# When q, k, v and the first expert's weights are loaded: in step order, or as early as buffers allow

## The chip, the cores and the metric

The kernel runs on one core of a Trainium2 chip. The metric is the device time of one launch in microseconds (us). The core has five engines, each with its own instruction stream: TensorE (PE in the profile), VectorE (DVE), ScalarE (ACT), GpSimd (POOL) and SyncE (SP). Transfers run on 16 DMA engines, which serve several queues. [...] The DMA transposes and the stores of the output are issued by SyncE (queue q1).

## The reference, cut to what matters

A block-sparse attention (a sorting network mixes the blocks of k and v) is followed by a mixture of experts whose gates are normalised in both directions.

```python
# attention: B=4, H=8, S=768, D=64, 8 blocks of 96 rows; P starts as sort_net
for _ in range(5):
    P = exp(P - max(P, -1)); P = P / (sum(P, -1) + 1e-9); P = P / (sum(P, -2) + 1e-9)
k_sorted = einsum('bhij,bhjcd->bhicd', P, k_b)
v_sorted = einsum('bhij,bhjcd->bhicd', P, v_b)
scores = matmul(q_b, k_sorted^T) / sqrt(D)          # inside each block
attn   = exp(scores - max); attn = attn / sum(attn)
x      = matmul(attn, v_sorted)                     # -> [3072, 512]

# experts: E=8, F=1024
P = exp(x @ w_gate - max)
for _ in range(8):
    P /= P.sum(1) + 1e-9;  P /= P.sum(0) + 1e-9;  P *= N / E
out = sum over e of  P[:, e] * (relu(x @ w1[e]) @ w2[e])
```

## The kernel before, in words

**Heads and pairs.** The 32 heads (4 batches of 8) are worked one after the other. q, k and v are loaded by pairs of heads: `load_pair(n)` (L65 to L73) takes a pair's buffer out of the pool `rawp`, which has six, and issues three DMAs of 192 KB each (bfloat16) from GpSimd, for k, v and q. `relayout(n)` (L75) reorders the pair's k and v on GpSimd into one of two `kv` buffers. `q_transpose(n)` (L253) turns q on TensorE into `qT_`.

**One step per head.** The loop at L399 goes over steps s = 0 to 33. Step s holds, in the order in which they are written: on even steps `build_R` for heads s+4 and s+5 (GpSimd, the sorting weights); `scores(s)`, on TensorE, with the maximum and the subtraction on VectorE (L327, L332, L334); the transpose of head s-1's weights on TensorE, with a copy on ScalarE (L349, L351); `sort_kv(s+2)`; `weights(s)`, the exponential on ScalarE (L338); on even steps `q_transpose(s//2+1)` and `relayout(s//2+2)`; `x_transpose` of a finished pair; `attend` of head s-1 (of head s-2 from head 16 on) with `normalise` (L356, L364, L365); the loads that the table `loads` names for this step; and, at s = 2, `load_expert(0)`.

**The ring around v.** `sort_kv(g)` (L306) sorts k and v of head g on TensorE, copies them to `kvT_` on ScalarE (L315), and SyncE issues a DMA transpose (L318) that writes v into `v1_`. `kvT_` has three buffers and `v1_` has five. The copy of head g+3 may start only when the transpose of head g has landed, and `attend(g)` needs that transpose too.

**Order.** The program is written out by hand (`manual_schedule`): each engine runs its own instructions in the order of the text. An instruction that waits holds back everything behind it on its engine. For GpSimd this means that loads, `build_R` and `relayout` stand in one queue. In front of the loop the kernel loads pairs 0 to 4 (L88 to L92), and after `relayout(1)` pair 5 and the gate's weights (L386, L387). The table (L396, L397) loads pairs 6 to 10 at steps 1, 3, 5, 7 and 9, and pairs 11 to 15 at steps 10, 11, 13, 15 and 17.

**The experts.** When a batch of heads is done, pieces of the gate and of expert 0's two layers (`gate_piece`, `l1_piece` L192, `l2_piece` L203) are put between the steps' work by `fill()`. The first pieces are added at the end of step 9 and run from step 10 on, so w1 of expert 0 is first read at 57.9 us and w2 at 67.3 us. Until step 8 the gaps on TensorE get `keep_warm` matmuls (L273) of no use to the result. After the heads come the rest of expert 0, the normalisation of the gates and experts 1 to 7 (L460, L538), from 186 us to the end.

Of the kernel before, what the change touches and what calls it, by code (L numbers as in the profile page):

```python
# [12 lines left out]
BF16 = mybir.dt.bfloat16  # L13
# [11 lines left out]
def kernel(  # L25
# [11 lines left out]
    nc = tc.nc  # L37
# [4 lines left out]
    N, Dm, E, F = 3072, 512, 8, 1024  # L42
# [22 lines left out]
    def load_pair(n):  # L65
        kv = rawp.tile([128, 2, 2, CL, D], BF16, name="kvr")
        qr = rawp.tile([128, 2, CL, D], BF16, name="qr")
        for t, r in ((k, kv[:, 0]), (v, kv[:, 1]), (q, qr)):
            nc.gpsimd.dma_start(
                out=r.rearrange("p h c d -> p h (c d)"),  # L70
                in_=bass.AP(tensor=t.tensor, offset=t.offset + 2 * n * S * D,
                            ap=[[CL * D, 128], [S * D, 2], [1, CL * D]]))
        raw_t[n] = (kv, qr)  # L73

    def relayout(n):  # L75

        kv = iop.tile([128, 2 * CL, 2, D], BF16, name="kv")
        nc.gpsimd.tensor_copy(kv.rearrange("p c t d -> p t c d"),  # L78
                              raw_t[n][0].rearrange("p t h c d -> p t (h c) d"))
        kv_t[n] = kv  # L80
# [8 lines left out]
    load_pair(1)  # L89
    load_pair(2)  # L90
    load_pair(3)
    load_pair(4)  # L92


    P9 = pp.tile([32, 9, 9], F32)
# [65 lines left out]
    wp = ctx.enter_context(tc.tile_pool(name="wp", bufs=2))  # L161
    wg = ones.tile([128, 4, E], BF16)
    w1t, w2t = [], []

    def load_expert(e):
        w1e = wp.tile([128, 4, F], BF16, name="w1e")
        w2e = wp.tile([128, 8, Dm], BF16, name="w2e")
        nc.gpsimd.dma_start(out=w1e, in_=moe_w1[e].rearrange("(kk k) f -> k kk f", k=128))  # L168
        nc.gpsimd.dma_start(out=w2e, in_=moe_w2[e].rearrange("(fb k) f -> k fb f", k=128))
        w1t.append(w1e)  # L170
        w2t.append(w2e)

    xtp = ctx.enter_context(tc.tile_pool(name="xtp", bufs=1))
    xtT = xtp.tile([128, 4, N], BF16)
# [63 lines left out]
    def fill():  # L238
        if slots[0] > 0:
            ahead[0] += sum(c for c, _ in pieces) / slots[0]  # L240
            slots[0] -= 1
        while pieces and ahead[0] >= pieces[0][0] / 2:
            c, run = pieces.pop(0)
            run()
            ahead[0] -= c
# [7 lines left out]
    def q_transpose(n):  # L253


        qr = raw_t[n][1]
        tq = psF.tile([128, 2, CL // 2, 128], BF16, name="psF")
        for e in range(2):
            for c in range(CL // 2):
                nc.tensor.matmul(tq[:, e, c], qr[:, e, 2 * c:2 * c + 2].rearrange("p l d -> p (l d)"),  # L260
                                 Ibf, is_transpose=True, start=True, stop=True)
        for e in range(2):
            to = qT_[0:64, n % 2, e, 0:S].rearrange(
                "p (i c l h) -> p l c i h", i=NB, l=2, h=CH)
            for l in range(2):
                (nc.vector.tensor_copy if e == 0 and n > 1 else nc.scalar.copy)(  # L266
                    to[:, l], tq[64 * l:64 * l + 64, e].rearrange("p c (i h) -> p c i h", h=CH))

    def keep_warm(n):

        w = psF.tile([128, 512], F32, name="psF")
        for i in range(n):
            nc.tensor.matmul(w[:, (i % 4) * 128:(i % 4 + 1) * 128], Ibf, Ibf, start=True, stop=True)  # L273
# [22 lines left out]
    def build_R(eng, src, g0, n):  # L296
        eng.tensor_tensor(
            out=R[:, g0:g0 + n],
            in0=mkap(src, [src.ap[0], [1, n], [32, 8], [0, CH]], off=g0),
            in1=mkap(mask16, [mask16.ap[0], [0, n], [0, 8], [1, CH]]),  # L300
            op=ALU.mult)
# [4 lines left out]
    def sort_kv(g):  # L306

        kv, e = kv_t[g // 2], g % 2
        kvps = psB.tile([128, 2, 512], F32, name="psB")
        kvf = mkap(kvps, [kvps.ap[0], [1, CL * 128]])  # L310
        for cl in range(CL):
            nc.tensor.matmul(kvf[:, cl * 128:(cl + 1) * 128],  # L312
                             kv[:, e * CL + cl].rearrange("p t d -> p (t d)"),
                             R[:, g].rearrange("p i c -> p (i c)"), start=True, stop=True)
        nc.scalar.copy(kvT_[:, g % NKT, :, 0:96].rearrange("p i (l c) -> p i l c", c=CH),  # L315
                       mkap(kvps, [kvps.ap[0], [CH, NB], [128, CL], [1, CH]]))

        nc.sync.dma_start_transpose(  # L318
            out=v1_[:, g % NVB, :, 0:64],
            in_=kvT_[64:128, g % NKT].rearrange("p i c -> p (i c)"))  # L320

    def scores(g):

        qT, kvT = qT_[:, (g // 2) % 2, g % 2], kvT_[:, g % NKT]
        sps = psB.tile([128, 2, 512], F32, name="psB")
        for i in range(NB):
            nc.tensor.matmul(sps[:, i // 4, (i % 4) * 96:(i % 4 + 1) * 96],  # L327
                             qT[:, i * BL:i * BL + 128], kvT[:, i, 0:96],
                             start=True, stop=True)
        s4 = sps[0:96, :, 0:384].rearrange("p a (i c) -> p a i c", c=96)  # L330
        mx = sp.tile([96, 2, 4], F32, name="mx")
        nc.vector.reduce_max(out=mx, in_=s4, axis=AX.X)  # L332
        ssb = sp.tile([96, 2, 4, 96], F32, name="ssb")
        nc.vector.tensor_sub(ssb, s4, mkap(mx, [mx.ap[0], [4, 2], [1, 4], [0, 96]]))  # L334
        ssb_t[g] = ssb

    def weights(g):
        nc.scalar.activation(out=at_[:, g % NAT, :, 0:96],  # L338
                             in_=ssb_t.pop(g).rearrange("p a i c -> p (a i) c"),
                             func=AF.Exp, scale=scale)  # L340
        if g in DT:
            nc.sync.dma_start_transpose(
                out=aT_[:, g % NTT, 0:S].rearrange("p (i c) -> p i c", c=BL),
                in_=at_[:, g % NAT].rearrange("p i c -> p (i c)"))

    def a_transpose(g):
        ta = psF.tile([128, NB, 96], BF16, name="psF")
        for i in range(NB):
            nc.tensor.matmul(ta[:, i, :], at_[:, g % NAT, i], Ibf[0:96, 0:96],  # L349
                             is_transpose=True, start=True, stop=True)  # L350
        nc.scalar.copy(aT_[0:97, g % NTT, 0:S], ta[0:97].rearrange("p i c -> p (i c)"))  # L351
# [31 lines left out]
    keep_warm(10)  # L383
    build_R(nc.gpsimd, Pb, 2, 2)
    relayout(1)
    load_pair(5)  # L386
    nc.gpsimd.dma_start(out=wg, in_=moe_w_gate.rearrange("(kk k) e -> k kk e", k=128))  # L387
    NP = NH // 2
    step = {g: g + (2 if g in DT else 1) for g in range(NH)}
# [3 lines left out]
    x_step = {}  # L393
    for n in range(NP):
        x_step.setdefault(max(step[2 * n], step[2 * n + 1]) + 1, []).append(n)
    loads = {2 * n - 11: n for n in range(6, 11)}  # L396
    loads.update({10: 11, 11: 12, 13: 13, 15: 14, 17: 15})  # L397
    new = []
    for s in range(NH + 2):  # L399
        if s % 2 == 0 and s + 4 < NH:  # L400
            build_R(nc.gpsimd, Pb, s + 4, 2)
        if s < NH:
            scores(s)
        if s == 0:
            sort_kv(1)
            onesc = ones.tile([128, 128], F32)
            nc.gpsimd.memset(onesc, 1.0)
            nc.gpsimd.memset(glog[:, NT, :], EPS / 128)
            nc.gpsimd.memset(glog[:, 0:NT, E:E + 1], EPS)
        fill()  # L410
        if s < 9:
            keep_warm(4)
        if 0 <= s - 1 < NH and s - 1 not in DT:
            a_transpose(s - 1)
        fill()
        if s + 2 < NH:
            sort_kv(s + 2)
        if s < NH:
            weights(s)
        if s % 2 == 0:  # L420
            if 0 < s and s // 2 + 1 < NP:
                q_transpose(s // 2 + 1)
            if s // 2 + 2 < NP:
                relayout(s // 2 + 2)
        for n in x_step.get(s, []):
            x_transpose(n)
            if n % 4 == 3 and n < NP - 1:
                new = [(0.7, gate_piece(n // 4))] + batch_pieces(n // 4)
        fill()
        if s < 9:  # L430
            keep_warm(6)
        for g in at_step.get(s, []):
            attend(g)
            normalise(g)
        if s in loads:
            load_pair(loads[s])
        fill()
        if new:
            add(new, {9:34,17:40,26:28}[s])
            new = []  # L440
        if s == 2:
            load_expert(0)
        if s == 31:

            late_ = pp.tile([1, 8], BF16)
            nc.gpsimd.tensor_copy(late_, at_[0:1, 31 % NAT, 0, 0:8])
            load_expert(1)
# [57 lines left out]
    for it in range(8):  # L505
# [8 lines left out]
            out=gl, in0=gl, scalar=float(N) / E,  # L514
# [5 lines left out]
    for e in range(1, E):  # L520
        if e + 1 < E:
            load_expert(e + 1)
        for nc4 in range(6):
            for fb in range(AHEAD if (e, nc4) == (1, 0) else 0, 8):
                l1_tile(e, nc4, fb)
            for tt in range(4):
# [8 lines left out]
                for c0 in range(0, Dm, W):  # L535
                    oacc = psF.tile([128, Dm], F32, name="psF")
                    for fb in range(8):
# [3 lines left out]
                        out=osbl[:, t, c0:c0 + W], in0=oacc[:, 0:W],  # L541
                        scalar=glog[:, t, e:e + 1], in1=osbl[:, t, c0:c0 + W],
                        op0=ALU.mult, op1=ALU.add)
                    if e == E - 1:
                        nc.sync.dma_start(out=out[t * 128:(t + 1) * 128, c0:c0 + W],
                                          in_=osbl[:, t, c0:c0 + W])
# [30 lines left out]
```

## Time and profile before

| what | us |
|---|---|
| median of 3 runs (760.49, 761.14, 768.26) | 761.14 |
| the profiled execution's own time | 764.39 |
| its span, first to last instruction | 762.6 |
| TensorE busy in the span | 736.4 (97%) |
| VectorE, ScalarE, GpSimd busy | 268.5, 331.9, 80.7 |
| first scores of head 0 (L327) | 15.8 |
| first piece of expert 0 (L192) | 57.9 |
| experts 1 to 7 from | 186 |

All times of places are counted from the start of the span of the profiled execution. A page of the profile shows busy times by engine, the span in 40 slices with the busy share of each in tenths, the DMA queues, the chain of work that ended last (followed back from the last instruction, each step to what released it), and groups of instructions. A row of the timeline has start, length, engine, line, operation, output and inputs, and, in brackets, how long the engine was idle before it and what ended that. In rows of a queue, the first number counts packets, the second is MB moved, the third the time that its packets took as a share of 16 engines.

### The profile page before, as it was taken

The page shows a single profiled execution, that of the slowest core. Times are in us where ns is not written, and L with a number is a line of the kernel's source. Part 1 is how long each engine was busy: PE and PEld are TensorE (multiplying, and loading weights), DVE is VectorE, ACT ScalarE, POOL GpSimd, SP SyncE. Part 2 cuts the span into 40 slices and gives each one's busy share as a digit, 9 for nine tenths or more (in the row PEclk, how much of TensorE's full clock was granted, in tenths as well). Part 3 has the DMA queues.
Part 4 walks back from the last instruction along what each step waited for, and adds up shares of the span by engine and source line. Part 5 has one row for each costly group of instructions (what it writes and reads, how often), then busy time and mean ns, then how long its engine had stood idle before and what let it go on. Part 6 is the DMA issues. An engine that isn't in the chain of part 4 may idle for free.

```text
span 762.6 us, 10716 instructions
## 1 busy us (share of the span) xinstructions
PE 736.4 (97%) x4509; PEld 375.3 (49%) x4509; DVE 268.5 (35%) x462; ACT 331.9 (44%) x559; POOL 80.7 (11%) x105
## 2 busy tenths in 40 slices
PE   6669999999999999999999999999999999999998
PEld 5657666655444444444444444444444444444444
DVE  5777888556512112122121221221212212112122
ACT  7778887744342332423424324233243342332422
POOL 8855430000000000000000000000000000000000
PEclk9999999999999999999999999999999999999999
DMA  9999656345100420015000700042001500002112
GB/s 151 159 176 179 110 91 81 61 86 91 21 1 1 74 37 1 0 28 83 1 0 1 111 0 1 1 65 46 1 0 20 92 0 1 1 1 96 70 70 96
DMA packets 58431, 40.15 MB, mean 53 GB/s; under 512 B 30608, under 2 KB 51344, under 8 KB 58384
## 3 DMA queue, kind: packets, MB, share of 16 engines
q0 software_dynamic: 26128, 26.23, 23.4%
q1 hardware_dynamic: 32256, 13.25, 8.5%
q8 instruction: 35, 0.57, 0.3%
q14 instruction: 12, 0.10, 0.0%
HBM read 52.45 MB, written 6.29 MB: 77 GB/s over the span
## 4 chain that ended last, share of the span: by engine, by line
PE 90%; DMA 4%; ACT 3%; DVE 2%; issue 1%; ACTq 0%; DVEq 0%
PE psF L538 38%; PE hps L460 38%; PE psF L203 5%; PE psF L192 5%; DMA v__108<-kvT__106 4%; PE psB L327 1%; ACT qT__111 L266 1%; PE psB L356 1%; PE psB L312 1%; ACT kvT__106 L315 1%; DVE ssb L334 1%; PE psF L349 0%; PE psF L374 0%; DVE mx L332 0%; PE psF L214 0%
## 5 line engine op out<-in xcount | busy, mean ns | idle before, releaser
L463 ACT ACTIVATE hTs<-hps 128x512 bf16<-128x512 f32 x336 | 200.8, 598 | 372.8 <-PE hps L460 372.8
L460 PE MATMUL hps<-xtT,w1e 128*128 128x512 bf16 x1344 | 297.4, 379 | 0.0
L538 PE MATMUL psF<-w2e,hTs 128*128 128x512 bf16 (+1 forms) x1352 | 296.9, 378 | 0.0
L540 DVE SCALAR_TENSOR_TENSOR osbl<-psF,glog,osbl 128x512 f32<-128x512 f32 (+1 forms) x169 | 126.3, 748 | 437.5 <-PE psF L538 437.4
L538 PEld LDWEIGHTS <-hTs 128*128 128x128 bf16 x1352 | 132.3, 98 | 157.8
L460 PEld LDWEIGHTS <-w1e 128*128 128x128 bf16 x1344 | 131.5, 98 | 158.5
L192 PE MATMUL psF<-xtT,w1e 128*128 128x384 bf16 x256 | 49.0, 325 | 0.6 <-ACT qT__111 L266 0.6
L168 POOL DMA_DIRECT2D w1e<-in_moe_w_dram x8 | 6.1, 767 | 394.3 <-PE hps L460 370.4
L203 PE MATMUL psF<-w2e,hTs 128*128 128x512 bf16 x192 | 45.4, 379 | 0.0
L195 ACT ACTIVATE hTs<-psF 128x384 bf16<-128x384 f32 x64 | 29.7, 499 | 7.4 <-PE psF L192 6.8
L315 ACT CAST kvT__106<-psB 128x768 bf16<-128x768 f32 x32 | 25.9, 808 | 16.1 <-issue 7.1
L332 DVE TENSOR_REDUCE mx<-psB 96x8 f32<-96x768 f32 x32 | 30.4, 949 | 5.3 <-PE psB L327 5.0
L334 DVE TENSOR_TENSOR ssb<-psB,mx 96x768 f32<-96x768 f32 x32 | 30.5, 954 | 3.2
L192 PEld LDWEIGHTS <-w1e 128*128 128x128 bf16 x256 | 22.9, 98 | 12.7 <-issue 1.0
L338 ACT ACTIVATE at__114<-ssb 96x768 bf16<-96x768 f32 x32 | 27.3, 853 | 2.0 <-DVE ssb L334 2.0
L203 PEld LDWEIGHTS <-hTs 128*128 128x128 bf16 x192 | 17.9, 100 | 17.0
L78 POOL COPY kv<-kvr 128x1536 bf16<-128x1536 bf16 x15 | 22.0, 1469 | 34.1 <-PE psB L312 17.5
L356 PE MATMUL psB<-v__108,aT__115 97*128 97x65 bf16 x256 | 13.1, 195 | 10.5 <-ACT kvT__106 L315 5.7
L365 DVE TENSOR_TENSOR og__309<-psB,den 96x512 bf16<-96x512 f32 x32 | 22.0, 687 | 1.1
L273 PE MATMUL psF<-Ibf 128*128 128x128 bf16 x169 | 16.7, 254 | 4.1 <-ACT Ibf L150 4.1
L356 PEld LDWEIGHTS <-aT__115 97*128 97x128 bf16 x256 | 11.7, 99 | 14.9 <-issue 12.2
L327 PE MATMUL psB<-kvT__106,qT__111 128*128 128x96 bf16 x256 | 16.5, 208 | 2.0 <-ACT kvT__106 L315 1.5
(84 smaller groups left out, 296.4 us busy)
## 6 DMA issues: line engine op xcount, KB each, us to landing
w1e<-in_moe_w_dram POOLq DMA_DIRECT2D x8, 1024.0 KB, 7.9
w2e<-in_moe_w_dram POOLq DMA_DIRECT2D x8, 1024.0 KB, 8.8
out_dram<-osbl SPq DMA_DIRECT2D x23, 256.0 KB, 2.0
kvr<-in_k_dram POOLq DMA_DIRECT2D x16, 192.0 KB, 8.1
kvr<-in_v_dram POOLq DMA_DIRECT2D x16, 192.0 KB, 8.7
qr<-in_q_dram POOLq DMA_DIRECT2D x16, 192.0 KB, 9.1
v__108<-kvT__106 SPq DMA_TRANSPOSE x32, 4.2
out_dram<-osbl SPq DMA_DIRECT2D x2, 128.0 KB, 1.7
```

Of the source, the lines that this page charges most:

```text
L192: nc.tensor.matmul(hps[:, 0:HC], w1t[0][:, kk, fb * 128:(fb + 1) * 128], xtT[:, kk, c * HC:(c + 1) * HC], start=(kk == 0), stop=(kk == 3))
L195: nc.scalar.activation(out=hT0[c][:, fb, 0:HC], in_=hps[:, 0:HC], func=AF.Relu)
L203: nc.tensor.matmul(oacc, hT0[c][:, fb, tt * 128:(tt + 1) * 128], w2t[0][:, fb, :], start=(fb == 0), stop=(fb == 7))
L315: nc.scalar.copy(kvT_[:, g % NKT, :, 0:96].rearrange("p i (l c) -> p i l c", c=CH), mkap(kvps, [kvps.ap[0], [CH, NB], [128, CL], [1, CH]]))
L332: nc.vector.reduce_max(out=mx, in_=s4, axis=AX.X)
L334: nc.vector.tensor_sub(ssb, s4, mkap(mx, [mx.ap[0], [4, 2], [1, 4], [0, 96]]))
L338: nc.scalar.activation(out=at_[:, g % NAT, :, 0:96], in_=ssb_t.pop(g).rearrange("p a i c -> p (a i) c"), func=AF.Exp, scale=scale)
L356: nc.tensor.matmul(ops_[:, i // 4, i % 4, 0:65], aT_[0:97, g % NTT, i * BL:i * BL + 128], v1_[0:97, g % NVB, i, 0:65], start=True, stop=True)
L460: nc.tensor.matmul(hps, w1t[e][:, kk, fb * 128:(fb + 1) * 128], xtT[:, kk, nc4 * 512:(nc4 + 1) * 512], start=(kk == 0), stop=(kk == 3))
L463: nc.scalar.activation(out=hT[e, nc4][:, fb, :], in_=hps, func=AF.Relu)
L538: nc.tensor.matmul(oacc[:, 0:W], hT[e, nc4][:, fb, tt * 128:(tt + 1) * 128], w2t[e][:, fb, c0:c0 + W], start=(fb == 0), stop=(fb == 7))
L540: nc.vector.scalar_tensor_tensor(out=osbl[:, t, c0:c0 + W], in0=oacc[:, 0:W], scalar=glog[:, t, e:e + 1], in1=osbl[:, t, c0:c0 + W], op0=A ...
```

## The change

Only the times of issue are changed. Pair 4 is loaded at step 2 instead of in front of everything, pair 5 at step 4 instead of before the loop. Pairs 6 to 10 are loaded at steps 6, 7, 8, 9 and 9 instead of 1, 3, 5, 7 and 9. Pairs 11 to 15 keep their steps. Expert 0's w1 is loaded at the end of step 1 and its w2 at the end of step 7, where both were loaded at the end of step 2. Buffers, sizes and all other instructions stay.

```diff
     load_pair(3)
-    load_pair(4)
...
+    def load_w1(e):
+        w1t.append(wp.tile([128, 4, F], BF16, name="w1e"))
+        nc.gpsimd.dma_start(out=w1t[e], in_=moe_w1[e].rearrange("(kk k) f -> k kk f", k=128))
+
+    def load_w2(e):
+        w2t.append(wp.tile([128, 8, Dm], BF16, name="w2e"))
+        nc.gpsimd.dma_start(out=w2t[e], in_=moe_w2[e].rearrange("(fb k) f -> k fb f", k=128))
+
     def load_expert(e):
-        w1e = wp.tile([128, 4, F], BF16, name="w1e")
-        w2e = wp.tile([128, 8, Dm], BF16, name="w2e")
-        nc.gpsimd.dma_start(out=w1e, in_=moe_w1[e].rearrange("(kk k) f -> k kk f", k=128))
-        nc.gpsimd.dma_start(out=w2e, in_=moe_w2[e].rearrange("(fb k) f -> k fb f", k=128))
-        w1t.append(w1e)
-        w2t.append(w2e)
+        load_w1(e)
+        load_w2(e)
...
     relayout(1)
-    load_pair(5)
     nc.gpsimd.dma_start(out=wg, in_=moe_w_gate.rearrange("(kk k) e -> k kk e", k=128))
...
-    loads = {2 * n - 11: n for n in range(6, 11)}
-    loads.update({10: 11, 11: 12, 13: 13, 15: 14, 17: 15})
+    loads = {2: [4], 4: [5], 6: [6], 7: [7], 8: [8], 9: [9, 10], 10: [11], 11: [12], 13: [13], 15: [14], 17: [15]}
...
-        if s in loads:
-            load_pair(loads[s])
+        for n in loads.get(s, ()):
+            load_pair(n)
         fill()
...
-        if s == 2:
-            load_expert(0)
+        if s == 1:
+            load_w1(0)
+        if s == 7:
+            load_w2(0)
```

## The prediction

> **What bounds the kernel now.** I read the page's slices first, then the chain of work that ended last.
>
> ```profile
> PE   6669999999999999999999999999999999999998
> ...
> DMA  9999656345100420015000700042001500002112
> ...
> PE 90%; DMA 4%; ACT 3%; DVE 2%; issue 1%; ACTq 0%; DVEq 0%
> ```
>
> One slice is 19 us. From the fourth slice on TensorE is full. In the first three it is at 0.6 while the DMA engines are at 0.9 or more. So the time is that of reaching the full stretch, plus TensorE's work from there. Between 57 and 186 us TensorE is busy for 126.20 of 129 us, and its waits there sum to some 4 us with no DMA among them. What is saved ahead of 57 us therefore reaches the end whole. The chain over 0 to 57 us, its longest pieces:
>
> ```profile
> 15.77 7.74 DMA v__108<-kvT__106
> ...
> 24.44 10.45 DMA v__108<-kvT__106
> ...
> 35.82 11.86 DMA v__108<-kvT__106
> ```
>
> Columns: start, length, what. These 30.05 us are three of the DMA transposes that line 318 issues, one per head, from SyncE. They lie on the chain because `kvT_` has three buffers: the copy of head g+3 (L315) waits until the transpose of head g has landed. The rows of L318 for 15 to 60 us and for 91 to 141 us, in this order, say what a transpose costs beside loads and without them:
>
> ```profile
> DMA to landing us min/median/max: 7.7/9.1/12.6
> ...
> DMA to landing us min/median/max: 2.5/2.5/4.4
> ```
>
> The queues in 34 to 36 us (expert 0's w1 is on the wires) and in 57 to 59 us (q, k, v loads), two lines each:
>
> ```profile
> q0 software_dynamic: 177, 0.36, 96.1%
> q1 hardware_dynamic: 153, 0.04, 15.3%
> ...
> q0 software_dynamic: 393, 0.28, 90.4%
> q1 hardware_dynamic: 389, 0.10, 36.7%
> ```
>
> First number: packets. Loads (q0) and transposes (q1) pass nearly one packet for one. From 15.5 to 87 us, q1 has 9792 packets for 18 transposes, 544 each. Beside loads they pass at 195 per us, so 2.8 us per transpose; beside w1 at 77 per us, 7.1 us; beside w2 (463 packets in 40 to 43 us) 3.5 us. A head goes by in about 3.3 us where nothing waits for a DMA, so beside loads that never pause the transposes only just keep up, and w1 puts them behind. The floor of a head is VectorE's:
>
> ```profile
> 28.58 0.20 DVE L364 RECIPROCAL den<-psB 96x8 f32<-96x8 f32 x1 [0.51 <-PE psB L356]
> ...
> 31.61 0.20 DVE L364 RECIPROCAL den<-psB 96x8 f32<-96x8 f32 x1 [0.19 <-PE psB L356]
> ...
> 35.47 0.20 DVE L364 RECIPROCAL den<-psB 96x8 f32<-96x8 f32 x1 [0.38 <-PE psB L356]
> ...
> 41.66 0.20 DVE L364 RECIPROCAL den<-psB 96x8 f32<-96x8 f32 x1 [3.27 <-PE psB L356]
> ```
>
> From one `den` to the next is one head: 3.03 us where VectorE hardly waits, 3.86, and 6.19 where it waits. With the two q copies (0.71 us, every second head) the same is 3.51 us (from 49.07 to 52.58), then 3.08. Floor: 3.05 and 3.5, in turn.
>
> **The change, part by part.**
>
> *What goes from the front.* The three loads of pair 4 leave the prologue and those of pair 5 leave the place after `relayout(1)`. Pair 3's q lands at 19.2 us with no load behind it but wg. Transpose 0, issued at 15.77, then finds free wires after 19.2 rather than loads until 23.5. I let it land at 20 to 22. Its two waiters move: the copy of head 3 (began 23.62, cannot begin before the ACT copy of 20.80 ends at 21.6) and the attend of head 0 (began 23.65, cannot begin before that copy either, 21.65). `den` of head 0 stood at 24.09; it becomes 22.1 at best, 22.9 if the wires stall as they do here.
>
> *The steps from there.* `den` of heads 0 to 8 now: 24.09, 28.58, 31.61, 35.47, 41.66, 45.35, 49.07, 52.58, 55.66. The differences are 4.49, 3.03, 3.86, 6.19, 3.69, 3.71, 3.51, 3.08. Against 3.5 and 3.05 in turn they are over by 1.0, 0, 0.35, 3.15, 0.2, 0.65, 0, 0: 5.35 us. With 1.2 to 2.0 at head 0 the most that can be gained is 6.6 to 7.4 us. What is late next is VectorE, so nothing beyond this is to be had without shorter steps.
>
> *w1 earlier.* It is issued at step 1 instead of step 2. POOL's queue: R and `relayout(1)` to 16.7, wg to 17.4 (pair 5's 2.2 us are gone), R, memsets and `relayout(2)` to 19.8, w1 there instead of at 26.03. Its row later in the kernel says 7.9 us to landing: about 28. From some 21.6 its packets meet whatever is left of transposes 1 and 2 (issued at 18.10 and 19.48), at 7.1 us per transpose. If those two are through by then, nothing is lost; if both are still whole, they land near 28.5 and 31, against copies due at about 25.5 and 28.5: 3 us lost. No row shows which. I take 0.9 us, nearer to nothing, because with free wires from 19.2 us two transposes need little more than what 24 to 28 us shows (1069 q1 packets there, two transposes, beside loads); range 0 to 3.
>
> *Loads in step order, and POOL.* Load n now stands behind `relayout(n-1)` on POOL, and that waits for the landing of n-1. With w1 landed at 28, pair 4's v lands at 30.2, `relayout(4)` (1.47 us) ends at 31.7; `sort_kv(8)` at step 6 wants it at 36.7. Load 5 is issued at 31.7, its v lands some 4.3 us after its issue (the second load of the kernel, from an empty queue) or a little more, `relayout(5)` ends near 38, due 43.2. Loads 6 and 7 and w2 are issued from 38 to 43.2, `relayout(6)` ends at 45.4, due 51.5. No engine waits; the slack is 5 us each time. The q halves land 5 us ahead of `q_transpose` (pair 4: 31.5 against 37).
>
> *w2 later.* The first use of w2 (L203) was at 67.31, so near 61 now. w2 goes out at 42.4 behind six loads of about 1.3 us each from 39.7, and takes some 7 us (46.66 less 39.1 here): landed at 54.5. Here POOL pays:
>
> ```profile
> 39.39 0.76 POOL L69 DMA_DIRECT2D kvr<-in_k_dram  x1 [0.35 <-DMA w1e<-in_moe_w_dram]
> 46.95 0.72 POOL L69 DMA_DIRECT2D kvr<-in_v_dram  x1 [6.80 <-DMA w2e<-in_moe_w_dram]
> ```
>
> A POOL load waits for the landing of the POOL load eight before it. That stall held back `relayout(6)` here. Counted in the new order, v of pair 10 is eight behind w2: it goes out at 54.6, q of pair 10 at 55.8, then R (0.66) and `relayout(7)`, which ends near 58.3. `sort_kv(14)`, 66.48 here, wants it at 60.1. Slack 1.8 us, cost nothing; if w2 lands 3 us later, 1 to 2 us are lost. I take 0.
>
> **The sum.** 7.3 (nearly the most) less 0.9 for w1: 6.4 us. The profiled execution took 764.39 us, its span 762.6, 1.8 around it; by its own time the result is 758.0. It lies 3.25 over the median of the runs, 761.14. The stretch in question has the same order in every run, so I take the 6.4 from the median: **754.7**.
>
> **Rivals.**
>
> *More than the floor* (a gain over 7.6, 753.5 or less). The floor rows themselves hold waits of 0.2 to 0.5 us, and TensorE's granted clock is 0.85 to 0.87 from 15.8 to 49 us against 1.00 later; steps of 2.95 and 3.4 would add 1 us. For: these waits; against: VectorE's own work is 2.8 us plus 0.71. Chance 0.25, 753.
>
> *w1 in the way of the first transposes, or `relayout(7)` late* (above): 2.5 to 4 us less. 758. Chance 0.18.
>
> *The wires stay as full.* All bytes remain, and what falls in steps 1 to 9 (w1, w2, pairs 4 to 7) is some 27 us of wire in 26 us. For it: beside loads a transpose still takes 2.8 us. Against: until now nine pairs and both weights ran in that time, and a pause of 2 us lets a backlog pass. Gain under 2: 761. Chance 0.07.
>
> *Loads too late: slower.* The place is the POOL chain landing, relayout, next load. The landing of v after its issue decides. At L us, `relayout(5)` ends at 33.8 + L, due 43.2, and `relayout(6)` at 36.0 + 2L, due 51.5: it bites from L = 7.7. In 47 to 61 us the loads took 9.4 to 12.1, median 10.4. At 10.4 `relayout(5)` is 0.8 late, `relayout(6)` a further 4.5, and w2, then landed at 67, holds `relayout(7)` until 71, a further 5.6: 10.9 late less the 6.4 is 4.5 slower, 765.6. Those rows had up to eight loads ahead in the queue, here there are two or three at most, so L is nearer to 5. Chance 0.09, and about half of it would be over 1%, with a landing of 12.
> [...]
>
> *The forecast* (a gain of 5 to 7.6): 0.41.
>
> **Range and chances.** 1% (7.6 us) is about what a measurement of this kernel can tell from no change. The forecast lies inside it, so "within 1%" holds the forecast, the second and third rival and half of the slower one: 0.69. Faster by over 1%: 0.25. Slower by over 1%: 0.06. The range leaves out a tenth at each end: the floor beaten by 1 us (752.5), and the late loads (above 761).
>
> **What would show it.** The chain no longer has transposes of 8 to 12 us in 15 to 48 us; copies L315 hardly wait for them; `den` steps at 3.0 and 3.5 from head 1 on; the first L192 at about 51.5 instead of 57.9; TensorE's clock at 1.00 there. Wrong would be: POOL's L78 copies ending later than the matmuls of L312 ask for, a wait of L312 on POOL, L203 waiting for w2, or transposes 1 to 3 landing after 28 us.

## The result, and the profile after

The changed kernel takes 764.73 us (median of 22 runs), the kernel before 761.71 us beside it: a ratio of 1.0034, 95% interval 1.0019 to 1.0049. It is slower by 0.3%. The prediction was 754.7 us, with a range from 752.5 to 761.0.

The profiled execution of the change took 764.50 us, with a span of 762.7. The slices of its page, and the shares of its chain:

```profile
PE   6778999999999999999999999999999999999998
...
DMA  9999945345100420015000600042001500002112
...
PE 90%; DMA 4%; ACT 3%; DVE 2%; issue 1%; POOL 1%; ACTq 0%; DVEq 0%; POOLq 0%
```

TensorE is fuller in the second and third slice (0.7 and 0.7, where before had 0.6 and 0.6) and emptier in the fourth (0.8, where before had 0.9), and the span is that of before. The DMA engines are busy for 0.9 of the fifth slice (76 to 95 us), where before had 0.6: the loads now have a fuller tail, which comes back below. At the front the transposes came sooner, as was expected, though some still took 8 to 10 us. Time to landing of the transposes of v issued from 15 to 50 us, before and after:

```profile
DMA to landing us min/median/max: 7.7/9.3/12.6
```

```profile
DMA to landing us min/median/max: 2.5/6.4/10.1
```

The rows of `den` on VectorE (L367 in the changed kernel), heads 8 to 11. First number: start.

```profile
49.04 0.20 DVE L367 RECIPROCAL den<-psB 96x8 f32<-96x8 f32 x1 [0.23 <-PE psB L359]
...
55.38 0.20 DVE L367 RECIPROCAL den<-psB 96x8 f32<-96x8 f32 x1 [0.72 <-PE psB L359]
...
59.59 0.20 DVE L367 RECIPROCAL den<-psB 96x8 f32<-96x8 f32 x1 [1.20 <-PE psB L359]
...
69.82 0.19 DVE L367 RECIPROCAL den<-psB 96x8 f32<-96x8 f32 x1
```

Head 8 comes at 49.04, where it came at 55.66. Head 11, at 69.82, is later than before (69.68). The 6.6 us are lost between heads 8 and 11. The chain of the change there (start, length, what):

```profile
41.69 5.55 DMA kvr<-in_v_dram
...
47.40 1.41 POOL kv L78
48.80 12.99 DMA kvr<-in_k_dram
...
62.82 0.66 POOL R L300
63.48 1.41 POOL kv L78
...
64.94 0.68 PE psB L315 x6
```

and the same on GpSimd's timeline, with TensorE's row behind it:

```profile
45.24 0.95 POOL L170 DMA_DIRECT2D w2e<-in_moe_w_dram  x1
...
53.71 0.72 POOL L69 DMA_DIRECT2D kvr<-in_k_dram  x1 [0.55 <-DMA qr<-in_q_dram]
60.66 0.71 POOL L69 DMA_DIRECT2D kvr<-in_v_dram  x1 [6.23 <-DMA w2e<-in_moe_w_dram]
62.09 0.71 POOL L69 DMA_DIRECT2D qr<-in_q_dram  x1 [0.71 <-DMA kvr<-in_k_dram]
62.82 0.66 POOL L300 TENSOR_TENSOR R<-Pb,mask 128x256 bf16<-128x256 f32 x1
63.41 1.47 POOL L78 COPY kv<-kvr 128x1536 bf16<-128x1536 bf16 x1
```

```profile
64.94 0.68 PE L315 MATMUL psB<-R,kv 128*128 128x128 bf16 x6 [3.40 <-POOL kv L78]
```

v of pair 10 waits on GpSimd for w2's landing (issued at 45.24, 15.13 us to landing, so 60.37), and q of pair 10 for the landing of k of pair 8 (issued at 48.80, 12.99 us, so near 61.8). Behind them stand R and `relayout(7)`, and behind that `sort_kv(14)`: TensorE idles for 3.40 us. Then a second loss, in TensorE's clock. Rows of the change: stretch, its length, TensorE's busy time (instructions), granted clock, DMA share, GB/s.

```profile
48.06:51.47 3.41, 1.86 (x49) 1.00 1.32 183
51.47:54.89 3.42, 3.42 (x20) 0.50 1.26 184
...
61.71:65.13 3.42, 0.19 (x4) 1.00 1.30 196
65.13:68.54 3.41, 3.41 (x18) 0.50 1.31 197
```

In both cases a stretch in which TensorE was not full (1.86 and 0.19 of 3.4 us) is followed by 3.41 us at half clock, and TensorE was full there, so that the loss is half of that by estimate, 1.7 us. From head 8 to head 9 it was 1.66 us (6.34 where before took 4.68), and after the idle time at 61 to 65 us about as much again. Sum: 6.62 less 1.66 is 4.96, 5.03 at head 10; less 3.40 and some 1.8, nothing is left at head 11.

One more thing has to be known to read the medians. The first profiled execution of before (764.39 us) lay 2.7 us over its median. The kernel before was therefore profiled a second time (below): 762.33 us, span 760.6. There head 8 comes at 52.11:

```profile
52.11 0.20 DVE L364 RECIPROCAL den<-psB 96x8 f32<-96x8 f32 x1 [0.24 <-PE psB L356]
```

So the lead of the change at head 8 is 3.1 us and not 6.6. It is still 3.05 us at head 10 (62.64 against 59.59), because this execution has a stretch of half clock of its own from 54.81 to 58.22. All of it is lost from head 10 to head 11, where TensorE waits for `relayout(7)`: by head 11 the lead has become a lag of 2.2 (67.62 against 69.82), and 2.1 us is what the spans differ by (760.6 and 762.7).

### The profile page after: what moved, and what is told of

The parts are those of the page before. It is cut to its first block, busy times and chain, and to the rows that moved or that the text cites. A ratio compares the mean times of both kernels' runs of the same rounds, so it can differ in the third digit from the quotient of the medians.

```text
span 762.7 us, 10721 instructions
## 1 busy us (share of the span) xinstructions
PE 737.1 (97%) x4509; PEld 374.2 (49%) x4509; DVE 268.4 (35%) x462; ACT 331.9 (44%) x559; POOL 80.8 (11%) x105
## 4 chain that ended last, share of the span: by engine, by line
PE 90%; DMA 4%; ACT 3%; DVE 2%; issue 1%; POOL 1%; ACTq 0%; DVEq 0%; POOLq 0%
PE psF L543 38%; PE hps L465 38%; PE psF L206 5%; PE psF L195 4%; DMA kvr<-in_k_dram 2%; DMA v__103<-kvT__101 1%; PE psB L330 1%; PE psB L315 1%; DMA kvr<-in_v_dram 1%; PE psB L359 1%; ACT kvT__101 L318 1%; POOL kv L78 1%; ACT qT__106 L269 0%; DVE ssb L337 0%; PE psF L352 0%
## 5 line engine op out<-in xcount | busy, mean ns | idle before, releaser
L195 PE MATMUL psF<-xtT,w1e 128*128 128x384 bf16 x256 | 50.1, 331 | 0.6 <-ACT qT__106 L269 0.6
L206 PE MATMUL psF<-w2e,hTs 128*128 128x512 bf16 x192 | 46.6, 386 | 0.0
L198 ACT ACTIVATE hTs<-psF 128x384 bf16<-128x384 f32 x64 | 29.7, 497 | 8.1 <-PE psF L195 7.5
L195 PEld LDWEIGHTS <-w1e 128*128 128x128 bf16 x256 | 23.1, 99 | 13.0 <-issue 1.5
L206 PEld LDWEIGHTS <-hTs 128*128 128x128 bf16 x192 | 18.2, 102 | 18.0 <-issue 1.6
L315 PE MATMUL psB<-R,kv 128*128 128x128 bf16 x192 | 17.1, 229 | 4.8 <-POOL kv L78 3.4
```

The costliest lines, as they stand in the source:

```text
L195: nc.tensor.matmul(hps[:, 0:HC], w1t[0][:, kk, fb * 128:(fb + 1) * 128], xtT[:, kk, c * HC:(c + 1) * HC], start=(kk == 0), stop=(kk == 3))
L198: nc.scalar.activation(out=hT0[c][:, fb, 0:HC], in_=hps[:, 0:HC], func=AF.Relu)
L206: nc.tensor.matmul(oacc, hT0[c][:, fb, tt * 128:(tt + 1) * 128], w2t[0][:, fb, :], start=(fb == 0), stop=(fb == 7))
```

## The experiments

The theory: the lead at head 8 is real and is lost where GpSimd's queue stands behind w2, and to half clock. The first rival: the wires carry the same bytes, so the lead is lost somewhere in any case. The second: the clock alone. All ratios below are to the kernel before, run beside each version; the pair of numbers behind a ratio is its 95% interval.

The start of `den` by head, and the span, in the profiled executions (us):

| kernel | head 8 | 10 | 11 | 15 | 16 | 17 | span |
|---|---|---|---|---|---|---|---|
| before, first profile | 55.66 | 64.62 | 69.68 | 87.45 | 94.17 | 97.47 | 762.6 |
| before, second profile | 52.11 | 62.64 | 67.62 | 85.41 | 92.12 | 95.42 | 760.6 |
| the change | 49.04 | 59.59 | 69.82 | 87.59 | 94.31 | 97.61 | 762.7 |
| pair 10 later, second profile | 49.02 | 59.55 | 64.54 | 82.31 | 91.70 | 96.88 | 762.0 |
| pair 10 later and dummy matmuls | 49.19 | 58.16 | 63.22 | 80.99 | 93.03 | 98.85 | 764.0 |
| the same, three pairs not loaded | 49.69 | 58.65 | 63.71 | 81.48 | 88.20 | 91.49 | 756.6 |

In these rows the span is head 17 plus 665.1 or 665.2 us. All differences lie ahead of head 17. Each row is one execution, and executions of one kernel differ by several us (22 of the kernel before lie between 760.27 and 768.26), so a row says where time goes and the medians say how much.

**Pair 10 behind `relayout(7)`.** Pairs 10, 11 and 12 go one step later, so that at step 10 R and `relayout(7)` are written ahead of pair 10's loads.

```diff
-    loads = {..., 9: [9, 10], 10: [11], 11: [12], 13: [13], ...}
+    loads = {..., 9: [9], 10: [10], 11: [11], 12: [12], 13: [13], ...}
```

> Theory: the 6.6 us won by head 8 are lost at two places: 1.7 us to a stretch of half clock at 51.5, and 5.1 us because GpSimd holds relayout(7) behind a load that waits for w2's landing (3.4 us of idle TensorE at sort_kv(14), then 3.4 us at half clock). With pair 10 issued behind relayout(7) the second loss goes: relayout(7) ends near 51, sort_kv(14) comes near 61.5, time 759.6 us, 0.997 of before. Rival, the wires: the bytes are not there in time in any order; L203 then waits for w2 (landed 60.4) or a later relayout is late, and the time stays at 764 to 765, 1.003 of before. Rival, the clock alone: no more than 1 us better than the change.

Measured: 764.57 us, ratio 1.0026 (1.0003 to 1.0049). The wait of L315 for GpSimd is gone, as the theory said, and the time did not move, as the first rival said. The third expectation, the clock alone, would allow this number too; the next runs part them. The first rival does not have the place right: L206 (`l2_piece`, L203 in the kernel before) did not wait for w2, and no relayout was late. This kernel's first profile was its fastest run (761.41 us, against a median of 764.57), so it was profiled again.

> Pair 10 behind relayout(7) alone, profiled once more, because its first profile (761.41 us) was the fastest of its runs. Theory: in an execution near its median of 764.6 us, TensorE waits at head 16 for the DMA transpose of the weights by 3 to 6 us, where the first profile has 1.1 us. Rival: the time is lost at another place.

Measured: 763.79 us, one execution. The longest of TensorE's waits in it that names a DMA (us in total, times, longest):

```profile
PE psB L359 <- DMA aT__110<-at__109: 3.1, 1, 3.1
```

The lead over the second profile of before is 3.1 us up to head 15 (82.31 against 85.41) and turns into a lag of 1.5 us by head 17. From head 16 on, the softmax weights are transposed by DMA. The first of these transposes took 8.98 us here, and TensorE's clock was half from 92.8 to 96.2 us, after the wait (eight matmuls of L195 took 2.43 us from 92.44 on, four of them 0.81 us at 97.67).

**Dummy matmuls in steps 9 and 10.** They fill TensorE's idle time ahead of 51 us.

```diff
+        if s == 10:
+            keep_warm(10)
         fill()
-        if s < 9:
+        if s < 10:
             keep_warm(4)
...
-        if s < 9:
+        if s < 10:
             keep_warm(6)
```

> Dummy matmuls also in steps 9 and 10, nothing else against the change. Theory: the half clock at 51.5 goes, but sort_kv(14) still waits for relayout(7) near 63.4 to 64.9, so the end does not move: 764.7 us, 1.004 of before. Rival, the clock alone: 3 us better, 761.5 us, 1.000 of before.

Measured: 764.65 us, 1.0030 (1.0013 to 1.0048), where the change has 764.73. The clock is 1.00 from 49 to 57 us, where the change has its stretch of half clock from 51.47 to 54.89, and L315 waits as long as in the change:

```profile
PE psB L315 <- POOL kv L78: 3.4, 1, 3.4
```

The wait ends when GpSimd is through with w2's landing and `relayout(7)`, and half clock is there at this place too (the clock is 0.91 from 57 to 75 us, which is 3.2 us at half). The profile is the fastest of this kernel's runs (763.21 us); w2 landed at 58.9 in it, 1.4 us earlier than in the change, and the span is 1.3 us shorter. The median is that of the change, so the clock alone as the cause is ruled out.

**Both edits.**

> Pair 10 behind relayout(7) and dummy matmuls in steps 9 and 10. Theory: both losses go, less some 0.5 us for the dummy matmuls of step 10: 758.3 us, 0.9955 of before. Rival, the wires: as with pair 10 moved alone, 764 us.

Measured: 765.68 us, 1.0047 (1.0033 to 1.0062), the slowest median of all, though its profile has the earliest head 15 of the table. The theory fell here: both losses are mended and the time is no better. A piece of its chain, and TensorE's row behind it:

```profile
80.89 11.44 DMA aT__110<-at__109
```

```profile
92.38 0.62 PE L359 MATMUL psB<-v__103,aT__110 97*128 97x65 bf16 x8 [5.58 <-DMA aT__110<-at__109]
```

The DMA transpose of head 16's weights, issued at 80.89, stands among the last loads and lands at 92.33. q of pair 15, the last load, lands at 92.32. In the first profile of before the same transpose was issued at 87.4, beside the very end of the loads, and took 3.3 us. In the two profiles of before the last load lands at 89.2 and 87.1, in the change at 89.6. In the three profiles that have pair 10 moved, all loads, and DMA transposes of weights from head 16 on, the wait at head 16 is longer the earlier head 15 comes: 1.1 us with head 15 at 83.25 (the first profile of pair 10 moved alone), 3.1 at 82.31, 5.6 at 80.99. Two stretches of half clock come with the longest (91.3 to 98.2 us; the clock is 0.83 from 90 to 110). Why the loads end late can be seen in what q0 carried (packets, MB, share) from 17 to 49 us, in the second profile of before and in the change:

```profile
q0 software_dynamic: 5692, 4.71, 99.7%
```

```profile
q0 software_dynamic: 3814, 3.05, 76.5%
```

1.7 MB less came in that time, and they had to come later. The same two kernels from 75 to 95 us:

```profile
q0 software_dynamic: 1280, 0.92, 35.7%
```

```profile
q0 software_dynamic: 2900, 2.09, 71.1%
```

With both edits it is 2.26 MB.

**Two tests of this second theory.** One takes the wires' load away: pairs 13, 14 and 15 are not loaded and compute with pair 12's data, so that part of the output is not the reference's.

```diff
     def load_pair(n):
+        if n >= 13:
+            raw_t[n] = raw_t[12]
+            return
```

> Pair 10 behind relayout(7), dummy matmuls in steps 9 and 10, and the loads of pairs 13, 14 and 15 left out (those pairs compute with pair 12's data, so the output is not the reference's; same work otherwise). Theory, the end of the loads: the wires are free from 80 us, the transpose of head 16's weights lands in 2.6 to 5 us and not in 11.4, TensorE does not wait for it: 757.5 to 759 us, 0.995 of before. Rival: the wait at head 16 is of another kind, the time stays at 765 us.

Measured: 758.41 us, 0.9951 (0.9933 to 0.9970), 7.3 us under the median of the same kernel with these loads (765.68). Time to landing of the first DMA transpose of weights, issued at 81.4:

```profile
DMA to landing us min/median/max: 2.7/2.7/2.7
```

The other leaves all loads and takes the transposes of heads 16 to 19 to TensorE. `DT` is the range of heads whose weights are transposed by DMA.

```diff
-    DT = range(16, NH - 2)
+    DT = range(20, NH - 2)
```

> Pair 10 behind relayout(7), dummy matmuls in steps 9 and 10, and the weights of heads 16 to 19 transposed on TensorE, as those of heads 0 to 15 are, instead of by DMA. Theory, the end of the loads: with both first losses mended the lead of 6.5 us reaches head 15 and is lost at head 16, whose DMA transpose (the first of the weights) stands 11.4 us beside the last loads, which end at 89 to 92 us in every order tried; taken off the wires it costs 4 x 0.34 us of TensorE and the lead stays: 759 us, 0.996 of before. Rival, VectorE and ScalarE: heads 16 to 19 are held by their own chain (waits for ssb and the copies), and the time stays at 765 us.

Measured: 760.00 us, 0.9965 (0.9941 to 0.9988). Both agree with the theory in the place and, but for 1 us in the second, in the size. Each has a rival under which the time stays at 765 us, and in neither did it. The first test leaves the work of VectorE and ScalarE as it was, so their chain is ruled out as what held head 16; the second changes it a little, because the copies of four heads' transposes are ScalarE's. A control asks whether dummy matmuls and the transposes on TensorE do it without the later loads; the version itself ran again beside it.

> The kernel before, with its loads as they were, dummy matmuls in steps 9 and 10, and the weights of heads 16 to 19 transposed on TensorE: a control for what these two edits give without the later loads. Theory: before does not wait at head 16 (its transpose takes 3.1 to 3.3 us), so the edits cost TensorE some 1.4 us and save at most one stretch of half clock (1.7 us): 761 to 763 us, 1.000. Rival: the two edits alone make the gain of the version that beats both, 759.5 to 760 us, 0.997.

> Pair 10 behind relayout(7), dummy matmuls in steps 9 and 10, heads 16 to 19 transposed on TensorE, for the second time, beside the control: 760.0 us, 0.9965 of before. If the control's rival is right, no faster than the control.

Measured: the control 762.54 us, 1.0002 (0.9982 to 1.0021); the version 759.87 us, 0.9961 (0.9941 to 0.9981). The two edits give nothing that can be told to the loads as they were. So the gain belongs to the later loads, once what they cost further on is removed: the queue behind w2, and the transpose at head 16. What the dummy matmuls alone add to it no run tells: none has the other two edits without them.

**Half as many transposes on TensorE** (`DT = range(18, NH - 2)`).

> Pair 10 behind relayout(7), dummy matmuls in steps 9 and 10, and only heads 16 and 17 transposed on TensorE. Theory: two transposes less on TensorE (0.7 us), but head 18's weights go to the wires at about 89, while the last loads end near 91: 759.5 to 761 us. If it is under 759, the loads' end no longer matters there.

Measured: 759.09 us, 0.9953 (0.9934 to 0.9972), the lowest median of a complete version, 3.3 us under the kernel before (762.43 beside it). It lies a little under the expected range and not under 759, so that whether the loads' end still matters there stays open. Against heads 16 to 19 the difference lies inside the intervals. In its profile, its slowest run (761.51 us), w2 itself is late: L206 waits for it for 1.8 us. So it does for 1.85 us in the second profile with heads 16 to 19 on TensorE (762.06 us, its slowest run too), and not in the first (759.44 us).

**w2 at step 5.**

```diff
-        if s == 7:
+        if s == 5:
             load_w2(0)
```

> Only w2 goes from step 7 to step 5. It lands near 48 and the load eight behind it is v of pair 8, issued near 50: GpSimd does not wait. Theory: relayout(7) in time, the 5.1 us come back less up to 1.5 us because pair 6 stands behind w2: 759.6 to 761 us, 0.997 to 0.999 of before. Rival, the wires: relayout(6) is late by more than 3 us and the time stays at 764 us.

Measured: 762.73 us, 1.0012 (0.9997 to 1.0027). Its median is some 2 us under that of the change, with intervals that overlap, and not the 4 to 5 expected. GpSimd did not wait for w2. But w2 (landed at 49.8) made the transposes of v late, up to 11.07 us; head 8 comes at 50.84, and two stretches of half clock follow (51.3 to 58.1 us; the clock is 0.64 from 49 to 57). The rival had the right edit and the wrong place: `relayout(6)` cost TensorE 0.35 us, not over 3, and the longer wait, 2.58 us, was at the attend of head 8. It names a copy to `kvT_`, and by the chain that copy waited for a transpose of v issued at 38.38, which w2 (issued at 35.66) made 11.07 us long:

```profile
50.40 0.40 PE L359 MATMUL psB<-v__103,aT__110 97*128 97x65 bf16 x8 [2.58 <-ACT kvT__101 L318]
...
54.85 0.82 PE L315 MATMUL psB<-R,kv 128*128 128x128 bf16 x6 [0.35 <-POOL kv L78]
```

**Fuller wires.** The dummy matmuls in steps 9 and 10 are in this version too.

```diff
-    loads = {2: [4], 4: [5], 6: [6], 7: [7], 8: [8], 9: [9, 10], 10: [11], 11: [12], ...}
+    loads = {0: [4], 2: [5], 4: [6], 5: [7], 7: [8], 8: [9], 10: [10], 11: [11], 12: [12], ...}
...
-        if s == 7:
+        if s == 6:
             load_w2(0)
```

> Loads a step or two earlier than in the change, so that the wires do not idle between 17 and 44 us: pair 4 at step 0, 5 at 2, 6 at 4, 7 at 5, w2 at 6, 8 at 7, 9 at 8, 10 at 10, 11 at 11, 12 at 12; dummy matmuls in steps 9 and 10. Theory: the loads end near 85 instead of 89 to 92, head 16's weights are transposed in time, but the transposes of v beside w1 cost 1 to 2 us of the lead: 758.5 to 761 us, 0.996 to 0.999 of before. Rival, wires full from the front are what costs: head 8 comes no earlier than before, 762 us or more.

Measured: 761.59 us, 0.9993 (0.9976 to 1.0009). The time lies between the theory's range and the rival's. The loads end at 85.6 us, as the theory said, and nothing waits at head 16. But head 8 comes at 52.39, no earlier than in the second profile of before, as the rival said: one transpose of v, issued while w1 was on the wires, held TensorE for 3.0 us at head 3. The front is bought with the tail here, or the tail with the front.

**The kernel before, again.**

> The kernel before, unchanged, profiled once more, because its first profiled execution (764.39 us) lies 2.7 us over the median. Theory: the stretches of half clock (at 24.9 and 41.9 there) fall otherwise, den of head 8 comes 1 to 3 us ahead of 55.7, and the rest follows. If head 8 is at 55.7 again, the difference lies elsewhere.

Measured: 762.33 us, one execution; its rows are in the table. Head 8 comes 3.55 us earlier than in the first profile, a little more than expected, and 2.0 us of that reach the end. The clock has three stretches of half clock ahead of 60 us here as there, one of them from 37.7 (the clock is 0.84 from 35 to 39 us) and one from 54.8. Its copies and attends wait less at the front: transpose 0 landed after 5.7 us where the first profile has 7.74, and `den` of head 0 stands at 22.29, against 24.09. In that first profile q0 and q1 passed 239 and 147 packets from 20 to 23 us, in the second 618 and 148. What slowed the loads there is not settled.

## Why the prediction was wrong

**What held.** The front was sized rightly against the profile that it was read from: head 8 was to come 6.4 us earlier and came 6.62 earlier, at steps of 3.1 and 3.5 us. w1 cost 0.56 us at most, where 0.9 was taken: head 0 to head 8 took 26.76 us (22.28 to 49.04), and the floor, four times 3.5 and 3.05, is 26.2. `relayout(4)`, `(5)` and `(6)` were in time, with 2.5 to 3.5 us to spare each (they ended at 33.45, 41.0 and 48.86, and the `sort_kv` that reads them began at 36.94, 43.52 and 52.41); the loads of q were in time. The rival of late loads as a chain of landing and relayout did not happen. That the 6.4 was met so closely is in part luck: it holds only against the one execution that it was read from.

**"The stretch in question has the same order in every run, so I take the 6.4 from the median": failed.** The order is the same and the waits are not. In a second execution head 8 of the kernel before comes at 52.11, and the lead is 3.1 us, not 6.4. The profile was known to lie 3.25 us over the median, and the second execution, 2.06 us faster, is faster in the very stretch that the gain was taken from. The best complete version gains 3.3 us by its median.

**"w2 later: cost nothing": failed, and in the change the whole lead goes here.** The wait was named with its place, eight loads back (v of pair 10, the eighth load behind w2, waited 6.23 us for it, as v of pair 9 did for 6.80 us in the first profile of before), and its price was wrong: w2 was to land at 54.5 and landed at 60.4. It was issued at 45.24 and not at 42.4, because w1 landed at 29.7 and v of pair 4 at 31.8 (28 and 30.2 were taken), v of pair 5 at 39.4; and the six loads ahead of it took 1.6 to 1.7 us each (1.3 was taken), so that q of pair 7 landed at 53.4. w2 itself took the 7 us. `relayout(7)` ended at 64.9 instead of 58.3. The slack of 1.8 us had all of this against it: TensorE waited for 3.40 us at `sort_kv(14)`.

**The half clock had no term.** The prediction counted slow clock among what could be won ahead of 49 us. It did not price the half clock that followed two idle times of TensorE in the full stretch: 1.66 us at 51.5 and about 1.8 at 65.1. With the wait of 3.4 that is 6.9 us, counted from the first profile of before. The second has a stretch of half clock there itself, so against it 5.2 us remain, the wait and the half clock behind it. The rival "`relayout(7)` late" had 2.5 to 4.

**"What is saved ahead of 57 us reaches the end whole": failed twice.** In the change the lead is lost at 61 to 65 us, as just told. With that mended there is a second place, which no run of the change itself shows. The view was that no wait of TensorE from 57 to 186 us names a DMA. That holds for the kernel before, whose loads are nearly over when head 16 needs the wires. With the loads drawn out and the steps drawn in, they meet: 3.1 and 5.6 us of wait in two kernels, none where three pairs were not loaded. Each of the two places is enough to keep the time from falling, which is why moving pair 10 alone changed nothing.

**Two slips in the sums,** which do not move the forecast. At a landing of 10.4 us `relayout(5)` would be 1.0 us late (33.8 and 10.4, against 43.2), not 0.8. And about half of the slower rival's 0.09 over 1% would leave 0.70 within 1%, not 0.69.

**"Loads too late: slower".** The runs agree with this rival in the outcome for the change as it stands (764.73 us beside 761.71), and by another route than its chain of landing and relayout: in the change no load of q, k or v came too late for its user. What came late was w2, the issue queue behind it, and, once that was mended, the free wires for a transpose at head 16. Once both were mended the later loads were the faster ones, by 3.3 us at best.

## What to carry to other kernels

Loads that are delayed do not leave the wires (here q0 carried 1.7 MB less from 17 to 49 us and 1.2 MB more from 75 to 95): look for the stage in which they then fall, and for the first transfer there that something waits for. In a queue that is worked in order, count which earlier transfer each load must wait for (here the one eight loads back), and keep short work that others need ahead of the load behind a long one. Before a gain is read from one profiled execution that lies over the median, profile it again: the excess may be the gain.

## What the runs showed of the hardware

In the profiles of before and of the change, half clock came in stretches of 3.41 us on a grid of that step. Ahead of 100 us they begin at 14.61, 24.85 and 41.92 us in the first profile of before and at 13.93, 51.47 and 65.13 in the change, which is 3, 5, 11 and 4 steps apart. Two of them came in a row with both edits and with w2 at step 5 (6.8 us). The grid lies otherwise in each of the three executions (a stretch begins at 14.61 us of the span in the first profile of before, at 54.81 in the second, at 13.93 in the change). Where TensorE was full, one cost 1.66 us, from head 8 to head 9 of the change. It came not only after idle stretches: TensorE was busy for 1.86 of 3.41 us (0.55) ahead of the one at 51.47, with no gap longer than 1.01 us, and in the second profile of before for 2.13 (0.62):

```profile
51.40:54.81 3.41, 2.13 (x51) 1.00 1.46 129
54.81:58.22 3.41, 3.41 (x27) 0.50 1.30 196
```

while the change kept full clock after 2.15 us in 44.65 to 48.06 and after 2.04 (0.60) in 17.34 to 20.75, and the first profile of before after 2.10 in 31.68 to 35.09. So the busy share of the stretch ahead does not tell alone whether half clock comes.

In the first profile of before, loads and transposes passed nearly one packet for one (393 of q0 and 389 of q1 beside loads of q, k and v from 57 to 59 us, 177 and 153 beside w1 from 34 to 36, 464 and 463 beside w2 from 40 to 43). The packets of q0 had 0.7, 2.0 and 1.0 KB there, by its MB over its packets, and the transposes were slower where they were larger: with w1, w2 and the loads of q, k and v, q0 carried 0.18, 0.16 and 0.14 MB per us, which is not far apart, and 77, 154 and 195 packets per us of the transposes passed beside them. A transpose of v took 2.5 us at the least without loads (91 to 141 us), 7.3 to 9.1 among loads of q, k and v (48 to 72 us), and up to 12.6 with w1 or w2 on the wires.
